# Expert weights asked for one block sooner, and the first blocks moved between the steps of routing

## The chip, the cores and the metric

The kernel runs on one core of one Trainium2 chip. The metric is the device time of one execution, in microseconds (us). A core has five engines with an instruction stream each: TensorE (PE, matmuls; its weight loads are PEld), VectorE (DVE), ScalarE (ACT), GpSimd (POOL) and SyncE (SP, which here issues nearly all DMAs; POOL issues the indirect ones). They wait for each other and for DMAs by semaphores.

## What is computed

Three layers follow each other on 2304 tokens: a retention layer (attention with decay), a dense layer of width 2048 with softplus, and a mixture of 8 experts of which each token uses two. The part that the change touches is the last:

```python
logits = x @ w_gate
noise_scale = np.log1p(np.exp(x @ w_noise))
noisy_logits = logits + noise_scale * noise
top2 = np.argpartition(-noisy_logits, 2, axis=1)[:, :2]
...
for e in range(E):
    for k in range(2):
        mask = top2[:, k] == e
        h = np.maximum(x[mask] @ w1[e], 0.0)
        out[mask] += top2_w[mask, k, None] * (h @ w2[e])
```

Which token goes to which expert is known only on the chip, while the kernel runs.

## The kernel before, in words

**Precision.** Every fp32 operand of a large matmul is split into two fp16 parts, and three products are summed. An expert's weights, so split, take 2 MB per half (w1 and w2, 128 partitions x 8192 fp16 each). They are prepared early on and stored in DRAM (`wsc`).

**Layers one and two** run through six tiles of 384 tokens: `g1` (line 281) and `g2` (line 312) alternate on TensorE. `logits` (line 403) and `ranks` (line 444) route a tile once it is done and scatter each token's number and weight into a table in DRAM.

**Blocks.** The experts' work is cut into blocks of 128 rows, each of one expert. `schedule` (line 496) computes on VectorE which expert each block has. It runs twice: list a, from the first five of six tiles, gives the first 5 blocks (`NBA`); list b gives the rest once the last tile is routed. A list holds for each block its column of the table, the place of its weights, its expert, and whether the expert is new.

**One block** i passes through these steps. `prep` (line 613): POOL copies the block's token numbers out of the loaded table (`ti`) and gathers the rows (`xr`), and SP transposes them by DMA (`xt`). `weights(i, half)` (line 600): SP reads three numbers of the list into registers and starts a load that is skipped where the expert isn't new. `e1` (line 628): 2 x 12 matmuls into `ph`; ScalarE and VectorE write the two fp16 parts `hr`; SP transposes them (`ht`). `e2` (line 648): 24 matmuls into `py`. `combine` (line 659): ScalarE scales `py` into `y`, POOL adds it to the output by an indirect DMA. `place` (line 596) reads the place of the weights into a register of TensorE.

**Order.** TensorE runs `e1(i)` and then `e2(i-3)`. After `ht` of block i, SP asks for the w1 of block i+3 and the w2 of block i, both of which TensorE reaches three blocks later. Weights have three places, used in turn by successive experts; line 681 lets a load for block n begin when block n-3 has finished its matmuls. Experts are taken large, small, large, small, so that a small one hides behind a large one. The first five blocks take PSUM from a pool in which `py` has one buffer and `ph` two (`eps`), the later ones from a pool with two of each (`eps2`). 41 blocks are in the main loop; if the routing makes more, two more run one after the other behind a branch (line 815).

The instructions are put into each engine's stream by a scheduler that follows the order in which they are written, moves one forward where it expects another to wait, and keeps what `behind` and `issue_after` tie together.

Of the kernel before, what the change touches and what calls it, by code (L numbers as in the profile page):

```python
# [10 lines left out]
F32 = mybir.dt.float32  # L11
F16 = mybir.dt.float16
I32 = mybir.dt.int32
# [4 lines left out]
ALU = mybir.AluOpType  # L18

B, H, S, D = 4, 8, 576, 64  # L20
NT, DM, FF = 2304, 512, 2048
NE, F2 = 8, 1024
P = 128
# [3 lines left out]
NTILE = NT // TT  # L27
KC = DM // P
NFB = FF // P
NBLK = 2 * NT // P + NE - 1  # L30
NB = NT // P
NBA = 5
NTAIL = 2
NCOL = NE * NB + NBLK

BIG = 4096
ROW = (slice(0, 64), slice(64, 128))
# [38 lines left out]
def body(ctx, tc, ins, out):  # L76
# [264 lines left out]

    X2 = dram.tile([NT, 2 * DM], F16, name="X2")
    table = dram.tile([P * NCOL, 4], I32, name="table")
    init = rt.tile([P, 17, 4], I32, name="init")
    nc.gpsimd.memset(init[:, :, 0:1], 0)
    nc.gpsimd.memset(init[:, :, 1:2], BIG)
    nc.gpsimd.memset(init[:, :, 2:4], 0)

    zero = rt.tile([P, DM // 4], F32, name="zero")
    nc.gpsimd.memset(zero, 0.0)  # L350

    def out_zero():
# [7 lines left out]
    wg = rt.tile([P, 2, KC, 16], F16, name="wg")  # L360

    def route_load():
        nc.sync.dma_start(out=table.rearrange("(p a c) f -> p a (c f)", p=P, c=17),
                          in_=init.rearrange("p (o c) f -> p o (c f)", o=1).to_broadcast([P, NCOL // 17, 68]))
        nc.sync.dma_start(out=noise, in_=ins["moe2_noise"].rearrange("(j p) e -> p j e", p=P))
        nc.sync.dma_start(out=wg32[:, :, 0:8], in_=ins["moe2_w_gate"].rearrange("(k p) e -> p k e", p=P))
        nc.sync.dma_start(out=wg32[:, :, 8:16], in_=ins["moe2_w_noise"].rearrange("(k p) e -> p k e", p=P))
        nc.scalar.activation(wg[:, 0], wg32, AF.Copy, scale=S_WG)
        nc.vector.scalar_tensor_tensor(out=wg[:, 1], in0=wg32, scalar=S_WG, in1=wg[:, 0], op0=ALU.mult, op1=ALU.subtract)
# [121 lines left out]

    POS = {}

    def schedule(first, n):
        X = mybir.AxisListType.X
        s = "a" if first else "b"

        def new(*shape, dt=F32, count=[0]):  # L500
            count[0] += 1
            return rt.tile([P, *shape], dt, name=f"sc{s}{count[0]}")

        def tt(shape, a, b, op, dt=F32):
            o = new(*shape, dt=dt)
            nc.vector.tensor_tensor(out=o, in0=a, in1=b, op=op)
            return o

        def ts(a, s1, s2, op0, op1=None, dt=F32):
            o = new(a.shape[1], dt=dt)  # L510
            nc.vector.tensor_scalar(o, a, s1, s2, op0=op0, **({"op1": op1} if op1 else {}))
            return o

        def red(a, op=ALU.add):
            o = new(a.shape[1])
            nc.vector.tensor_reduce(out=o, in_=a, axis=X, op=op)
            return o

        inner = lambda a, m: a[:, None, :].to_broadcast([P, m, NE])
        outer = lambda a: a[:, :, None].to_broadcast([P, a.shape[1], NE])  # L520
        eid, num = iota[:, :NE], iota[:, :n]
        pc = ps.tile([P, NE], F32, tag="sm", name="pc", bufs=1)
        nc.tensor.matmul(pc, lhsT=ones, rhs=MC[NTILE - 1 if first else NTILE][:, 0], start=True, stop=True)
        ni = ts(pc, 0.0 if first else 127.0, None, ALU.add, dt=I32)
        nb = new(NE)
        nc.vector.tensor_copy(nb, ts(ni, 7, None, ALU.logical_shift_right, dt=I32))
        if first:
            key = new(NE)
            nc.vector.scalar_tensor_tensor(out=key, in0=pc, scalar=8.0, in1=eid, op0=ALU.mult, op1=ALU.subtract)
            pos = red(tt([NE, NE], inner(key, NE), outer(key), ALU.is_gt, F16))  # L530
            r1 = ts(pos, 2.0, None, ALU.mult)
            POS["pos"] = tt([NE], r1, ts(r1, -1.0, 15.0, ALU.mult, ALU.add), ALU.min)
            POS["done"] = None
        else:
            pos = POS["pos"]
            nb = tt([NE], nb, POS["done"], ALU.subtract)
        lt = tt([NE, NE], inner(pos, NE), outer(pos), ALU.is_lt, F16)
        some = ts(nb, 0.0, None, ALU.is_gt)
        before_b = red(tt([NE, NE], lt, inner(nb, NE), ALU.mult, F16))
        before_e = red(tt([NE, NE], lt, inner(some, NE), ALU.mult, F16))  # L540
        end = tt([NE], before_b, nb, ALU.add)
        last = ts(red(some[:, None, :]), -1.0, None, ALU.add)
        sel = tt([n, NE], outer(num), inner(before_b, n), ALU.is_ge, F16)
        sel = tt([n, NE], sel, tt([n, NE], outer(num), inner(end, n), ALU.is_ge, F16), ALU.subtract, F16)
        pick = lambda a: red(tt([n, NE], sel, inner(a, n), ALU.mult, F16))
        e = pick(eid)

        w = new(NE)
        nc.vector.scalar_tensor_tensor(out=w, in0=eid, scalar=float(NB), in1=before_b, op0=ALU.mult, op1=ALU.subtract)
        if not first:  # L550
            w = tt([NE], w, POS["done"], ALU.add)
        col = pick(ts(w, float(-NE * NB), None, ALU.add))
        bi = rt.tile([P, 4, n], I32, name="bi" + s)
        nc.vector.scalar_tensor_tensor(out=bi[:, 0], in0=col, scalar=float(NE * NB), in1=num, op0=ALU.add, op1=ALU.add)

        d = ts(pick(ts(before_e, last, None, ALU.subtract)), last, None, ALU.add)
        if first:
            POS["e"], POS["d"] = e[:, n - 1:n], d[:, n - 1:n]
            POS["done"] = tt([NE], ts(before_b, -1.0, float(n), ALU.mult, ALU.add), nb, ALU.min)
            nc.vector.tensor_scalar(POS["done"], POS["done"], 0.0, None, op0=ALU.max)  # L560
            nc.vector.memset(bi[:, 3, 0:1], 1)
        else:
            other = tt([1], e[:, 0:1], POS["e"], ALU.not_equal)
            nc.vector.tensor_copy(bi[:, 3, 0:1], other)
            d = ts(d, tt([1], other, POS["d"], ALU.add), None, ALU.add)
        three = tt([n], ts(d, 3.0, -3.0, ALU.is_ge, ALU.mult), ts(d, 6.0, -3.0, ALU.is_ge, ALU.mult), ALU.add)
        nc.vector.tensor_tensor(out=bi[:, 1], in0=three, in1=d, op=ALU.add)
        nc.vector.tensor_copy(bi[:, 2], e)
        nc.vector.tensor_tensor(out=bi[:, 3, 1:], in0=d[:, 1:], in1=d[:, :n - 1], op=ALU.is_gt)
        if not first:  # L570
            LIST["more"] = ni[0:1, 0:1]
            nc.vector.tensor_scalar(ni[:, 0:1], red(nb[:, None, :]), float(n - NTAIL), None, op0=ALU.is_gt)
        tab = E["ep"].tile([P, NCOL * 4], I32, name="tab", bufs=1)
        nc.sync.dma_start(out=tab, in_=table.rearrange("(p c) f -> p (c f)", p=P))
        return bi, tab
# [94 lines left out]
    def weight_deps():  # L670

        for W, M in ((W1, M1), (W2, M2)):
            for n, w in W.items():
                need(M[n][0], w)
                for i in (n - 1, n - 2):
                    if i >= 0:
                        for m in M[i]:
                            tc.declare_no_dep(w.ins, m.ins, reason="another place")
                            tc.declare_no_dep(m.ins, w.ins, reason="another place")
                if n >= 3:  # L680
                    need(w, M[n - 3][-1], mybir.DependencyReason.ANTI)
                for i in W:
                    if i < n:
                        tc.declare_no_dep(w.ins, W[i].ins, reason="another place, or an expert already used")
# [92 lines left out]
        step()  # L777
    for g in sorted(todo):
        run(g)
    logits(NTILE - 1)  # L780
    ranks(NTILE - 1)
    LIST["b"] = schedule(False, NBLK - NBA)
    ps_s.close()
    E["eps2"] = ctx.enter_context(tc.tile_pool(name="eps2", bufs=2, space=bass.MemoryType.PSUM, side="right"))
    LAG, AHEAD = 3, 3
    NMAIN = NBLK - NTAIL
    preps = list(range(PA, NMAIN))
    for i in range(NMAIN + LAG):
        j = i - LAG

        def second():
            e2(j)
            combine(j)
            if j + 3 < NMAIN:
                weights(j + 3, 1)

        early = i == NMAIN - 1
        if early:
            second()
        if i < NMAIN:  # L800
            e1(i)
            if i == 0:
                weights(i, 1)
            if i + 1 < NMAIN:
                place(i + 1)
            if i + 3 < NMAIN:
                weights(i + 3, 0)
        if j >= 0 and not early:
            second()
        while preps and preps[0] <= i + AHEAD + 1 and (preps[0] < NBA or i >= PB):  # L810
            prep(preps.pop(0))
            if preps and preps[0] == NBA + 2 and i == PB:
                break
# [36 lines left out]
```

## Time and profile before

| | us |
|---|---|
| median of 3 runs (lowest, highest) | 962.01 (955.81 to 967.28) |
| the profiled execution | 956.63 |
| its span in the trace | 954.8 |
| TensorE busy in the span | 907.2 (95%) |
| VectorE, ScalarE, GpSimd busy | 384.8, 375.3, 262.0 |
| mean granted TensorE clock | 0.982 |

TensorE is busy through most of the span, so time is to be found where it stands still or runs at a lower clock. The profiled execution lies near the lowest of the three runs. Rows of the trace name line and engine, then what is written `<-` what is read.

### The profile page before, as it was taken

Reading aid. Unit: us, or ns where it says so; the run is one execution under the profiler, and the core shown is the slowest. Engines: PE = TensorE matmul, PEld = TensorE weight load, DVE = VectorE, ACT = ScalarE, POOL = GpSimd, SP = SyncE. Lnnn points to the kernel's source line nnn. Section 1 sums busy time; section 2 is a strip of 40 time slices with the busy share of each in tenths; the row PEclk is TensorE's granted clock in tenths of the full one; section 3 lists DMA queues with packets and bytes.
Section 4 is the critical chain, followed back from the end, with each engine's and each line's share of the span. In section 5 each row is a group of like instructions: output and inputs, shape, how many; then the busy total and the mean of one; then the engine's idle time right before and its main releaser. Section 6 shows DMA issues by size and latency. Waiting matters only on the chain. (4 is left out here: it accounts for less than half of the span.)

```text
span 954.8 us, 17453 instructions
## 1 busy us (share of the span) xinstructions
PE 907.2 (95%) x5690; PEld 464.4 (49%) x5690; DVE 384.8 (40%) x757; ACT 375.3 (39%) x601; POOL 262.0 (27%) x237
## 2 busy tenths in 40 slices
PE   7788899999999999999997999999999999899996
PEld 6444455555555555555543444444444444344442
DVE  4576775777867876424445111111111111111100
ACT  2777774665766766344431111111111111111111
POOL 3367632401410310200222223223222322223112
PEclk8899998999999999999999999999999999999999
DMA  9768899999999999003067777799879999999873
GB/s 311 249 227 276 218 281 326 309 358 327 343 326 321 355 363 272 1 1 67 18 179 206 150 132 124 150 243 213 216 138 198 212 235 185 199 268 219 213 174 54
DMA packets 221428, 206.70 MB, mean 216 GB/s; under 512 B 159360, under 2 KB 169216, under 8 KB 219296
## 3 DMA queue, kind: packets, MB, share of 16 engines
q1 hardware_dynamic: 211008, 185.29, 69.7%
q0 software_dynamic: 10336, 20.27, 11.6%
q8 instruction: 54, 0.88, 0.4%
q14 instruction: 30, 0.25, 0.1%
HBM read 245.70 MB, written 54.20 MB: 314 GB/s over the span
## 5 line engine op out<-in xcount | busy, mean ns | idle before, releaser
L637 PE MATMUL ph<-w,xt 128*128 x984 | 223.4, 383 | 9.2 <-DMA w<-wsc 5.7
L654 PE MATMUL py<-w,ht 128*128 x984 | 219.2, 379 | 2.0 <-ACT y L665 1.9
L281 PE MATMUL pg<-x,wi 128*128 128x384 f16 x1152 | 208.7, 331 | 5.3 <-POOL wi L151 3.2
L312 PE MATMUL p<-w,g 128*128 128x512 f16 x864 | 203.8, 383 | 10.3 <-POOL w L151 8.3
L642 DVE SCALAR_TENSOR_TENSOR hr<-ph,hr 128x512 f16<-128x512 f32 x82 | 56.7, 691 | 361.0 <-ACT hr L641 346.9
L637 PEld LDWEIGHTS <-xt 128*128 128x128 f16 x984 | 96.7, 98 | 127.5 <-issue 15.3
L281 PEld LDWEIGHTS <-wi 128*128 128x128 f16 x1152 | 112.6, 99 | 92.4 <-issue 6.8
L654 PEld LDWEIGHTS <-ht 128*128 128x128 f16 x984 | 96.2, 98 | 118.7 <-issue 2.9
L666 POOL DMA_INDIRECT out_dram<-y,ti x41 | 65.3, 1592 | 303.0 <-ACT y L665 274.3
L312 PEld LDWEIGHTS <-g 128*128 128x128 f16 x864 | 81.2, 98 | 103.3 <-issue 14.6
L641 ACT ACTIVATE hr<-ph 128x512 f16<-128x512 f32 x82 | 49.0, 597 | 178.4 <-PE ph L637 176.6
L665 ACT ACTIVATE y<-py,ti 128x512 f32<-128x512 f32 x41 | 28.2, 687 | 187.1 <-PE py L654 182.6
L335 DVE SCALAR_TENSOR_TENSOR w<-w 128x1024 f16<-128x1024 f32 x64 | 86.0, 1347 | 30.0 <-ACT w L334 29.8
L334 ACT ACTIVATE w<-w 128x1024 f16<-128x1024 f32 x64 | 67.4, 1057 | 53.4 <-DMA wsc<-w 28.2
L290 ACT ACTIVATE r<-pg 128x384 f32<-128x384 f32 x96 | 46.6, 485 | 99.2 <-PE pg L281 99.0
L295 DVE SCALAR_TENSOR_TENSOR r<-a,r 128x768 f32<-128x768 f32 x48 | 49.0, 1021 | 75.0 <-ACT a L294 74.7
L482 POOL DMA_INDIRECT table<-tb,pos x36 | 41.8, 1160 | 124.7 <-DVE pos L467 99.9
L621 POOL DMA_INDIRECT xr<-X,ti x41 | 43.4, 1060 | 19.6 <-POOL ti L618 11.6
L210 POOL TENSOR_TENSOR w<-kv,w 96x512 f32<-96x512 f32 x19 | 21.0, 1107 | 98.6 <-PE pst L239 54.7
L291 ACT ACTIVATE a<-pg 128x384 f32<-128x384 f32 x96 | 46.6, 485 | 0.0
L213 POOL TENSOR_TENSOR w<-qk,w 128x384 f32<-128x384 f32 x20 | 24.5, 1226 | 66.7 <-PE px L258 45.4
L293 ACT ACTIVATE a<-a 128x768 f32<-128x768 f32 x48 | 40.3, 841 | 1.2
(126 smaller groups left out, 607.1 us busy)
## 6 DMA issues: line engine op xcount, KB each, us to landing
w<-wsc SPq DMA_DIRECT2D x78, 2048.0 KB
w<-in_moe_w_dram SPq DMA_DIRECT2D x64, 512.0 KB
wsc<-w SPq DMA_DIRECT2D x64, 512.0 KB
qk<-in_qk_dram SPq DMA_DIRECT2D x24, 384.0 KB
kv<-in_kv_dram SPq DMA_DIRECT2D x24, 384.0 KB
w<-in_moe_w_in_dram SPq DMA_DIRECT2D x8, 1024.0 KB
w<-in_moe_w_out_dram SPq DMA_DIRECT2D x8, 1024.0 KB
out_dram<-zero SPq DMA_DIRECT2D x1, 4608.0 KB
```

The source lines that it names most:

```text
L281: nc.tensor.matmul(pg, lhsT=wi[:, a, k, f * P:(f + 1) * P], rhs=x[:, b, k, :], start=n == 0, stop=n == 11)
L290: nc.scalar.activation(r[:, i], pg, AF.Relu, scale=S_G / sx)
L291: nc.scalar.activation(a[:, i], pg, AF.Abs)
L295: nc.vector.scalar_tensor_tensor(out=r, in0=a, scalar=S_G, in1=r, op0=ALU.mult, op1=ALU.add)
L312: nc.tensor.matmul(PG[t, j], lhsT=g[:, a, f % 2, j * P:(j + 1) * P], rhs=wo[b][:, f, :], start=f == 0 and a + b == 0, stop=f == NFB - 1 an ...
L334: nc.scalar.activation(h[:, 0], t, AF.Copy, scale=s)
L335: nc.vector.scalar_tensor_tensor(out=h[:, 1], in0=t, scalar=s, in1=h[:, 0], op0=ALU.mult, op1=ALU.subtract)
L637: M1[i].append(nc.tensor.matmul(ph, lhsT=xt[:, a * 4 + k, :], rhs=AR[0][:, ds(r * 8192 + (b * 4096 + k * 1024 + n * 512), 512)], start=m = ...
L641: LAST["act"] = nc.scalar.activation(hr[:, 0, n * 512:(n + 1) * 512], ph, AF.Relu)
L642: nc.vector.scalar_tensor_tensor(out=hr[:, 1, n * 512:(n + 1) * 512], in0=ph, scalar=0.0, in1=hr[:, 0, n * 512:(n + 1) * 512], op0=ALU.max ...
L654: M2[i].append(nc.tensor.matmul(py, lhsT=ht[:, a * 8 + c, :], rhs=AR[1][:, ds(r * 8192 + (b * 4096 + c * 512), 512)], start=len(M2[i]) == ...
L666: LAST["pool"] = nc.gpsimd.indirect_dma_start(out=out[:, :], out_offset=bass.IndirectOffsetOnAxis(ap=ti[:, 1:2], axis=0), in_=y[:, :], in_ ...
```

## The change

Four edits. (1) A load for block n is asked for one block sooner: w1 of block i+4 after `e1(i)`, w2 of block j+4 after `e2(j)`; it then waits for the matmuls of block n-4 instead of n-3. (2) List b gives each of the four largest experts at least two blocks if it has any left; the tail grows to three blocks, the table by some columns, and the modulo of the place by a term. There are still three places. (3) Blocks 0 to 2 are written between the steps of routing: `e1(0)` after `logits`, `e1(1)` after `ranks`, and `e1(2)` inside the second `schedule`, by the argument `between`. (4) Two small constant tiles move to a pool that is closed later on.

```diff
-NBLK = 2 * NT // P + NE - 1
+NBLK = 2 * NT // P + NE
-NTAIL = 2
-NCOL = NE * NB + NBLK
+NTAIL = 3
+NCOL = NE * NB + NBLK + 2
...
+            POS["least"] = ts(pos, 4.0, 1.0, ALU.is_lt, ALU.add)
...
             nb = tt([NE], nb, POS["done"], ALU.subtract)
+            nb = tt([NE], nb, tt([NE], ts(nb, 0.0, None, ALU.is_gt), POS["least"], ALU.mult), ALU.max)
...
         sel = tt([n, NE], sel, tt([n, NE], outer(num), inner(end, n), ALU.is_ge, F16), ALU.subtract, F16)
+        between()
...
+        three = tt([n], three, ts(d, 9.0, -3.0, ALU.is_ge, ALU.mult), ALU.add)
...
-                if n >= 3:
-                    need(w, M[n - 3][-1], mybir.DependencyReason.ANTI)
+                if n >= 4:
+                    need(w, M[n - 4][-1], mybir.DependencyReason.ANTI)
...
-    logits(NTILE - 1)
-    ranks(NTILE - 1)
-    LIST["b"] = schedule(False, NBLK - NBA)
...
+    def first(i):
+        e1(i)
+        place(i + 1)
+    logits(NTILE - 1)
+    first(0)
+    weights(0, 1)
+    weights(3, 0)
+    weights(3, 1)
+    weights(4, 0)
+    ranks(NTILE - 1)
+    first(1)
+    prep(preps.pop(0))
+    LIST["b"] = schedule(False, NBLK - NBA, lambda: first(2))
...
+    weights(5, 0)
+    weights(6, 0)
+    for i in range(2, NMAIN + LAG):
...
-            if j + 3 < NMAIN:
-                weights(j + 3, 1)
+            if j + 4 < NMAIN:
+                weights(j + 4, 1)
...
-            if i + 3 < NMAIN:
-                weights(i + 3, 0)
+            if i + 4 < NMAIN:
+                weights(i + 4, 0)
```

Two places of the streams, as they stand in the two kernels. VectorE before, towards the end of the second `schedule` (`scb...` are its intermediate values, `bib` is list b): the two `hr` rows of block 1 stand behind nearly all of it.

```order
L572 TENSOR_SCALAR scb1_5356<-scb34_5428 128x1
L564 CAST bib_5402<-scb28_5412 128x1
L506 TENSOR_TENSOR scb29_5415<-scb28_5412,sca31_4952 128x1
L642 SCALAR_TENSOR_TENSOR hr_5525<-ph_5526,hr_5525 128x512
L511 TENSOR_SCALAR scb30_5417<-scb27_5410,scb29_5415 128x38
L642 SCALAR_TENSOR_TENSOR hr_5525<-ph_5541,hr_5525 128x512
```

VectorE in the changed kernel: the same two rows stand at the beginning of the second `schedule`, right behind the positions (`pos`) that `ranks` computes, and the two of block 2 further on within it.

```order
L465 SCALAR_TENSOR_TENSOR qi_5428<-qi_5428 128x6
L467 SCALAR_TENSOR_TENSOR pos_5434<-qi_5428 128x6
L649 SCALAR_TENSOR_TENSOR hr_5460<-ph_5461,hr_5460 128x512
L512 TENSOR_SCALAR scb1_5521<-pc_5519 128x8
L649 SCALAR_TENSOR_TENSOR hr_5460<-ph_5476,hr_5460 128x512
L512 TENSOR_SCALAR scb3_5524<-scb1_5521 128x8
L527 CAST scb2_5523<-scb3_5524 128x8
```

What moved: block 1's two `hr` come ahead of the schedule's some 35 small operations instead of behind them, and what is left of the schedule comes behind them.

SP before, at the same point (`w2` is the load of block 0's second half, `tab` the table for list b):

```order
L645 DMA_TRANSPOSE ht_5468<-hr_5437 128x16x128
L609 ISA
L609 REGISTER_ALU
L609 DMA w2_85<-wsc_87 128x8192
L574 DMA tab_5431<-table_89 128x748
L605 TENSOR_LOAD bia_4944
```

SP in the changed kernel, later: the load of `tab` has moved behind the skipped loads of blocks 3 and 4 and behind the transposes of blocks 1 and 2.

```order
L616 DMA w1_84<-wsc_87 128x8192
L652 DMA_TRANSPOSE ht_5491<-hr_5460 128x16x128
L652 DMA_TRANSPOSE ht_5590<-hr_5559 128x16x128
L581 DMA tab_5648<-table_89 128x760
L612 TENSOR_LOAD bib_5615
```

What moved: the table is fetched later, behind two transposes that stood behind it; the load of block 0's second half still follows the transpose of block 0. Further on the two streams have the same pattern (transpose of `hr`, a load for each half, transpose of `xr`), with the loads belonging to one block later than before.

## Rows read from the trace of the kernel before

**Rows 1.** Waits of TensorE, 480 us to the end: engine, line, releaser: us, times, longest.

```profile
PE ph L637 <- DMA w<-wsc: 5.7, 3, 4.6
...
PE ph L637 <- DVE hr L642: 3.6, 1, 3.6
...
PE py L654 <- ACT y L665: 1.9, 2, 1.0
```

**Rows 2.** Timeline of TensorE, first blocks: start, us, engine, line, operation [idle before].

```profile
512.68 3.61 PE L637 MATMUL ph<-w,xt 128*128 x16
...
519.85 7.03 PE L637 MATMUL ph<-w,xt 128*128 x24 [3.56 <-DVE hr L642]
...
526.72 5.13 PE L654 MATMUL py<-w,ht 128*128 x23
...
538.29 2.75 PE L654 MATMUL py<-w,ht 128*128 x12 [1.05 <-ACT y L665]
...
549.64 1.02 PE L654 MATMUL py<-w,ht 128*128 x4 [0.83 <-ACT y L665]
```

**Rows 3.** Windows, core 0: PE, PEld, DVE, ACT, POOL busy, clock, DMA share, GB/s.

```profile
516.30:519.85 3.55, 0.00 (x0) 0.00 (x0) 3.55 (x16) 0.60 (x1) 2.64 (x4) 1.00 0.96 402
...
520.00:521.00 1.00, 1.00 (x5) 0.41 (x4) 0.97 (x5) 0.00 (x0) 0.81 (x1) 0.87 0.79 330
...
521.00:522.00 1.00, 1.00 (x4) 0.34 (x3) 0.31 (x2) 0.00 (x0) 0.89 (x1) 0.50 0.12 22
```

**Rows 4.** Timeline of TensorE, later blocks.

```profile
757.30 5.34 PE L637 MATMUL ph<-w,xt 128*128 x24 [0.30 <-DMA w<-wsc]
...
788.38 5.34 PE L637 MATMUL ph<-w,xt 128*128 x24
...
793.86 5.34 PE L654 MATMUL py<-w,ht 128*128 x24
...
824.55 7.00 PE L637 MATMUL ph<-w,xt 128*128 x24 [4.64 <-DMA w<-wsc]
...
831.39 5.34 PE L654 MATMUL py<-w,ht 128*128 x24
...
899.63 5.34 PE L637 MATMUL ph<-w,xt 128*128 x24 [0.74 <-DMA w<-wsc]
```

**Rows 5.** Timeline of SP's queue, later blocks.

```profile
735.62 0.64 SPq L609 DMA_DIRECT2D w<-wsc  x2
...
747.23 0.90 SPq L609 DMA_DIRECT2D w<-wsc  x2
...
798.58 2.00 SPq L645 DMA_TRANSPOSE ht<-hr  x1
...
812.76 0.94 SPq L609 DMA_DIRECT2D w<-wsc  x2
...
815.66 9.21 SPq L645 DMA_TRANSPOSE ht<-hr  x1
...
890.72 0.91 SPq L609 DMA_DIRECT2D w<-wsc  x2
```

**Rows 6.** Timeline of VectorE, end of the second schedule.

```profile
519.12 0.68 DVE L642 SCALAR_TENSOR_TENSOR hr<-ph,hr 128x512 f16<-128x512 f32 x1
...
521.11 0.23 DVE L567 TENSOR_TENSOR bib<-scb,scb 128x38 int32<-128x38 f32 x1
```

**Rows 7.** Timeline of SP and GpSimd, list b and block 5.

```profile
513.98 0.59 SPq L609 DMA_DIRECT2D w<-wsc  x1
...
523.27 0.32 SPq L574 DMA_DIRECT2D tab<-table  x1
...
526.13 0.19 POOL L618 COPY ti<-tab 128x4 int32 x1 [4.04 <-DMA tab<-table]
...
535.95 2.62 SPq L625 DMA_TRANSPOSE xt<-xr  x2
```

More of the change, by code (lines that the diff above doesn't have):

```diff
@@ L343, in body @@
     table = dram.tile([P * NCOL, 4], I32, name="table")
-    init = rt.tile([P, 17, 4], I32, name="init")
+    init = ap.tile([P, 19, 4], I32, name="init", bufs=1)
     nc.gpsimd.memset(init[:, :, 0:1], 0)
@@ L347, in body @@
     nc.gpsimd.memset(init[:, :, 2:4], 0)
-    zero = rt.tile([P, DM // 4], F32, name="zero")
+    zero = ap.tile([P, DM // 4], F32, name="zero", bufs=1)
     nc.gpsimd.memset(zero, 0.0)
@@ L362, in route_load @@
     def route_load():
-        nc.sync.dma_start(out=table.rearrange("(p a c) f -> p a (c f)", p=P, c=17),
-                          in_=init.rearrange("p (o c) f -> p o (c f)", o=1).to_broadcast([P, NCOL // 17, 68]))
+        nc.sync.dma_start(out=table.rearrange("(p a c) f -> p a (c f)", p=P, c=19),
+                          in_=init.rearrange("p (o c) f -> p o (c f)", o=1).to_broadcast([P, NCOL // 19, 76]))
         nc.sync.dma_start(out=noise, in_=ins["moe2_noise"].rearrange("(j p) e -> p j e", p=P))
@@ L494, in body, with schedule @@
     POS = {}
-    def schedule(first, n):
+    def schedule(first, n, between=lambda: None):
         X = mybir.AxisListType.X
@@ L674, in weight_deps @@
                 need(M[n][0], w)
-                for i in (n - 1, n - 2):
+                for i in (n - 1, n - 2, n - 3):
                     if i >= 0:
@@ L779, in body @@
         run(g)
-    logits(NTILE - 1)
-    ranks(NTILE - 1)
-    LIST["b"] = schedule(False, NBLK - NBA)
-    ps_s.close()
-    E["eps2"] = ctx.enter_context(tc.tile_pool(name="eps2", bufs=2, space=bass.MemoryType.PSUM, side="right"))
     LAG, AHEAD = 3, 3
@@ L787, in body @@
     preps = list(range(PA, NMAIN))
-    for i in range(NMAIN + LAG):
+    def first(i):
[11 more added lines that the diff above has]
+    LIST["b"] = schedule(False, NBLK - NBA, lambda: first(2))
+    ps_s.close()
+    E["eps2"] = ctx.enter_context(tc.tile_pool(name="eps2", bufs=2, space=bass.MemoryType.PSUM, side="right"))
+    weights(5, 0)
+    weights(6, 0)
+    for i in range(2, NMAIN + LAG):
         j = i - LAG
@@ L799, in body @@
             second()
-        if i < NMAIN:
+        if 2 < i < NMAIN:
             e1(i)
-            if i == 0:
-                weights(i, 1)
             if i + 1 < NMAIN:
                 place(i + 1)
-            if i + 3 < NMAIN:
-                weights(i + 3, 0)
+            if i + 4 < NMAIN:
+                weights(i + 4, 0)
         if j >= 0 and not early:
```

## The prediction, on record before the changed kernel ran

> **What bounds it now.** I read the page first: TensorE is busy for 95% of the span, so whatever is won must come from its pauses or from its clock. Then the list of TensorE's waits from 480 us on [rows 1]: three waits for an expert's weights, 5.7 us together, one of 3.6 us for VectorE, and two of 1.9 us together for ScalarE. Nothing else there is in reach of this change, so the prize is small from the start; the timelines show what each pause really costs.
>
> In the first blocks [rows 2], block 1's last matmuls start at 512.68 and end at 516.29. Block 2 starts only at 519.85: its PSUM buffer is freed by VectorE, whose `hr` of block 1 stands behind the second schedule and runs at 519.12 [rows 6]. TensorE has nothing else to do meanwhile, and when it starts again its granted clock is at the lower level, 1.2 GHz (0.50), where it was at 2.4 GHz (1.00) before the pause [rows 3]. So the group of 24 matmuls takes 7.03 us, against 5.34 in the later groups [rows 2, 4]. The reader should see that one pause is paid twice.
>
> In the later blocks [rows 4], groups of 24 last 5.34 us, but the last one overlaps its successor, and undisturbed starts follow each other by 5.18 us (5.34 less the 0.16 of overlap). Three experts' first blocks start late (757.30, 824.55, 899.63), with 0.30, 4.64 and 0.74 us of idle; the overlap that is lost adds 0.16 to each. The group at 793.86 follows the one at 788.38 by 5.48, thus 0.30 late. After the longest pause the clock is low again: 824.55 to 831.39 is 6.84, or 1.66 over 5.18.
>
> Why the weights are late stands in SP's queue [rows 5]. The loads come in pairs, one pair for each block. The pair that carries w1 of block 31 goes out at 812.76, 7 us before TensorE wants it. A transpose issued behind such a load takes 9.21 us instead of 2.00, so SP runs behind: from 747.23 to 890.72 are 13 pairs, 11.04 us each, against 10.36 (two groups of 5.18) for a block on TensorE.
>
> **The change, part by part.**
>
> *The first blocks.* VectorE now writes `hr` of block 1 as soon as it is there. Block 2 can start at 516.3, and its clock stays up. That removes 3.56 us and 7.03 - 5.34 = 1.69 us [rows 2]. The new order has one second matmul group directly behind another in the pool with a single `py` buffer, where it had two pauses for that buffer, 1.05 and 0.83 us: I keep the first and take away the second. Sum: 3.56 + 1.69 + 0.83 = 6.1 us.
>
> Two things could eat this. First, `e2(0)`, which now follows block 2, moves from 526.72 to about 516.3 + 5.2 = 521.5, and needs block 0's w2, issued at 513.98 [rows 7]. DMA moves 330 GB/s between 520 and 521 us and only 22 in the next [rows 3], so the load lands at about 521.1: just in time. The bounds are nothing lost, and 526.5 - 521.5 = 5 us lost, since before it had landed when `e2(0)` started. I take nothing, by the drop in traffic.
>
> Second, what is left of the schedule waits for two further `hr` of block 2, and list b, ready at 521.3 [rows 6], is ready about 5 us later, 526.6 by my count of its operations. Block 5 hangs on it: from `ti` at 526.13 to `xt` at 535.95 was 9.8 us [rows 7]. Now POOL first adds block 0's output, so `ti` comes near 530 and `xt` near 540, with some 3 us until it has landed. In the new order of TensorE block 5 comes after five groups for blocks 3, 4, 0, 1 and 2 from 521.5, at about 548.5. A cover of some 5 us is left; if it is gone, what is missing is paid in full. The three further operations of the first schedule, and four of the second, cost 0.1 to 0.2 us each on VectorE; the latter are in the 526.6, the former shift a wait by less than 0.5 us, which I leave out.
>
> *The loads, one block sooner.* They make up 0.46 + 0.30 + (4.64 + 0.16 + 1.66) + 0.90 = 8.1 us [rows 4]. Are they soon enough? Up to 735.62 SP keeps up with TensorE, and so it gets the 6.1 us from the first blocks as well. From there the same pairs follow in the same mixture, one block sooner; that is 747.23 - 735.62 = 11.6 us [rows 5]. Block 31's w1 goes out at 812.76 - 11.6 - 6.1 = 795.1 and needs 824.55 - 812.76 = 11.8 us: 806.9. It is wanted at 819.75 - 6.1 - 0.8 = 812.9. Margin 6.0. Block 38's goes out at 890.72 - 17.7 = 873.0, needs 899.63 - 890.72 = 8.9, so 881.9; wanted at 898.73 - 6.1 - 7.2 = 885.4. Margin 3.5, or 0.6 if it needs 11.8 too. So all four go, with little to spare at the end.
>
> What is not free is the place in the queue. Each load now stands ahead of the transpose of an older block than before, and a transpose behind a load takes 9.21 us instead of 2.00 [rows 5], 7.2 more. The transpose of block 29, out at 824.87, is used three blocks later, at 841.75 or so (819.75 + 4.80 + 1.66 + 3 x 5.18), with 17 us of cover; the shift takes 7.2 of that, the gain of TensorE over SP's queue up to 7.2 more. That leaves 2 to 3 us, so I cost it at nothing. The Trainium skill, "DMA: Bandwidth & Descriptors", section "Queues, rings and completion order", says that on each DMA engine a queue's descriptors are consumed in ring order. By that rule alone the transposes pay for what the loads win, and the sum would be that of the rival "transposes late" below; the trace agrees with the order (9.21 against 2.00 us), but not with there being no cover.
>
> *At least two blocks for a large expert; three tail blocks.* The reference, run on its own inputs, gives the eight experts 148, 573, 208, 22, 292, 1614, 1033 and 718 tokens, so 2 + 5 + 2 + 1 + 3 + 13 + 9 + 6 = 41 blocks, with a new expert at blocks 13, 14, 23, 25, 31, 33 and 38; the late ones of [rows 4] are three of these. The four largest have 8, 9, 6 and 5 blocks in list b, so the rule adds none, the list stays at 41 and the tail is jumped over as before: nothing. The table's columns and the two moved constants: nothing, they are written in the first microsecond or moved by DMA beside matmuls.
>
> **Sum.** 6.1 + 8.1 = 14.2 us, against the profiled execution's 956.63: 942.4, or 1.5% less. The median of the runs, 962.01, lies 5.4 higher; what those runs lost I cannot see, so I subtract the same: 947.8, rounded to **948 us**.
>
> **The rivals.**
>
> *Weights still late, or SP the next bound.* For: SP needs 11.04 us a block where TensorE needs 10.36 [rows 4, 5], 13 x 0.68 = 8.8 us over that stretch, so a queue that is behind can give back what the earlier asking wins. Against: the margins above. If 5 of the 8.1 remain, 962.0 - 9.2 = 952.8.
>
> *The first blocks win nothing.* The wait for VectorE is replaced by one for block 0's w2 or for block 5's rows. For: covers of 0.4 and 5 us only. Then 962.0 - 8.1 = 953.9.
>
> *Both, in part*, or the pauses of the profiled execution are not those of the other runs: 957 to 963, no change.
>
> *Transposes late: slower.* Each load pushes a transpose by 7.2 us; where the cover of 17 us in the later blocks is used up, `e2` waits at each load and the clock falls after it. It decides once SP is 17 us further behind TensorE than now. Then the seven loads among those 13 pairs would cost 7 x 7.2 = 50 us less the 14.2 won: 962 + 36 = 998; two more than the win, 963 to 975, are likelier than all.
>
> *The change does not do what it says:* extra blocks run the tail. With 41 blocks counted it cannot for these inputs; I give it 0.01, within the case of slower.
>
> **Chances and range.** Forecast 0.60 (944 to 952); weights or SP 0.15; first blocks 0.10; both in part 0.09; slower 0.06. The range must hold 0.8: the forecast, most of the next two, and 2 us less than the forecast's lowest if the other runs' extra 5.4 us lie in these same pauses (962.0 - 14.2 - 5.4 = 942.4). So 941 to 957. About 1% is what a measurement of this kernel can tell from no change, so faster means under 952.4: 0.58 of the forecast's 0.60, and half of the next two, 0.12, together 0.70. Slower by over 1% is 0.05 of the 0.06. Within 1%: the remaining 0.25.
>
> **What would show it.** In the new trace: no idle at block 2's first matmuls and a clock of 1.00 there; `e2(0)` at about 521.5 with no wait for `w<-wsc`; block 5 unhindered; no wait for `w<-wsc` at blocks 25, 31 and 38; pairs in SP's queue about 17 us sooner than before late in the list. Wrong if a wait of `py` for `ht` appears in the later blocks, if list b delays block 5, or if the time saved at these places is lost in the first 480 us, where I predict no difference.

## The result and the profile after

The changed kernel takes **948.72 us**, the median of 6 runs (944.47 to 952.0); the kernel before, run beside it, 961.75 (6 runs). The ratio is 0.9851, with a 95% interval of 0.9813 to 0.9889: 1.5% faster, as forecast to the microsecond. The traces show that the forecast was luckier than its working: what it counted went, but of its 14.2 us some 9.4 came back elsewhere in the execution that was profiled. (A run more than 1.5% above the fastest of its kernel is left out of the ratios in this document, not out of the medians.)

That execution took 951.07 us, 2.4 above the median of its runs; the one of before lay 5.4 below its median. So the two traces differ by 5.6 us only, and the medians by 13.0. From the first block's first matmul to the end of the span they differ by 6.0 (453.65 and 447.6 us).

First the waits of TensorE from 480 us on, after (compare [rows 1]; columns as there):

```profile
PE ph L644 <- DMA xt<-xr: 3.9, 1, 3.9
...
PE py L661 <- DMA ht<-hr: 1.3, 1, 1.3
PE py L661 <- issue: 1.2, 1, 1.2
PE py L661 <- ACT y L672: 0.8, 1, 0.8
```

All three waits for weights are gone, the one for VectorE's `hr` and one of the two for ScalarE too. New are waits for the two transposes, `xt` and `ht`, which no row of before has. Their places, in TensorE's timeline after:

```profile
512.17 4.04 PE L644 MATMUL ph<-w,xt 128*128 x18
...
516.08 5.34 PE L644 MATMUL ph<-w,xt 128*128 x24
522.62 5.34 PE L661 MATMUL py<-w,ht 128*128 x24 [1.21 <-issue]
527.80 10.52 PE L644 MATMUL ph<-w,xt 128*128 x48
...
544.34 5.34 PE L661 MATMUL py<-w,ht 128*128 x24 [0.84 <-ACT y L672]
549.51 10.52 PE L644 MATMUL ph<-w,xt 128*128 x48
...
851.45 5.34 PE L661 MATMUL py<-w,ht 128*128 x24 [1.33 <-DMA ht<-hr]
...
861.80 5.34 PE L661 MATMUL py<-w,ht 128*128 x24
871.06 7.94 PE L644 MATMUL ph<-w,xt 128*128 x24 [3.91 <-DMA xt<-xr]
878.84 1.46 PE L661 MATMUL py<-w,ht 128*128 x6
...
894.38 5.34 PE L644 MATMUL ph<-w,xt 128*128 x24
```

Block 2 follows block 1 with no pause, in 5.34 us where it took 7.03 after 3.56 of idle [rows 2]. `e2(0)` starts 1.2 us late. Blocks 5 and 6 (549.51) are not held up. `e1(38)`, the first block of the last new expert, starts at 894.38 with no wait. At 851.45 `e2(31)` waits for its `ht`; at 871.06 `e1(36)` for its `xt`, and its 24 matmuls then take 7.94 us: the clock is paid a second time, as at block 31 before [rows 4]. The clock's side, in the windows over block 2 and over `e1(36)` (columns as in [rows 3]):

```profile
516.08:521.42 5.34, 5.34 (x26) 2.25 (x24) 4.50 (x20) 1.20 (x2) 4.12 (x5) 1.00 0.86 349
871.06:878.84 7.78, 7.78 (x25) 3.01 (x25) 0.69 (x1) 0.60 (x1) 2.68 (x3) 0.66 1.06 160
```

1.00 is 2.4 GHz; the mean of 0.66 comes from a first part at 1.2 GHz (0.50 in the windows up to 876 us). And SP's queue after (compare [rows 5]):

```profile
794.49 1.10 SPq L616 DMA_DIRECT2D w<-wsc  x2
...
832.31 9.18 SPq L652 DMA_TRANSPOSE ht<-hr  x1
...
853.86 1.15 SPq L616 DMA_DIRECT2D w<-wsc  x2
855.13 1.40 SPq L632 DMA_TRANSPOSE xt<-xr  x1
856.63 13.98 SPq L652 DMA_TRANSPOSE ht<-hr  x1
873.15 0.64 SPq L616 DMA_DIRECT2D w<-wsc  x2
...
881.13 0.91 SPq L616 DMA_DIRECT2D w<-wsc  x2
```

Block 31's w1 goes out at 794.49 (812.76 before), 18.3 us sooner. Block 38's goes out at 881.13 (890.72 before), only 9.6 us sooner. The pair of 873.15 is the one before it, and both its loads are skipped: SP's queue moves 0.79 MB from 872 to 881 us, less than one load of 2 MB, and 2.73 MB from 881 to 892. For the two late transposes, these are the rows of the kernel before, of SP's queue and of the TensorE steps that read them:

```profile
837.31 7.10 SPq L645 DMA_TRANSPOSE ht<-hr  x1
...
862.40 1.26 SPq L625 DMA_TRANSPOSE xt<-xr  x1
```

```profile
862.47 5.34 PE L654 MATMUL py<-w,ht 128*128 x24
...
878.01 5.34 PE L637 MATMUL ph<-w,xt 128*128 x24
```

After, the `xt` of block 36 comes behind the pair of 853.86. It is asked at 855.13 and is there when TensorE goes on, at about 871: 16 us. TensorE's step before it ended at 861.80 + 5.34 = 867.1. The `ht` of block 31, asked at 832.31, took until about 851.4. Before, these two were asked at 862.40 and 837.31: the change brings them forward by 7.3 and 5.0 us, the load of block 31 by 18, and TensorE would reach the two steps 11.0 and 12.5 us sooner than before (`e1(36)` stood at 878.01, `e2(31)` at 862.47; now due at 866.98 and 849.95).

The DMA packets show where the 16 us of `xt` go. A load moves in large packets and a transpose in small ones. From 856.4 to 862 us only 10 of 144 packets were under 512 bytes, and SP's queue moved 1.79 MB; from 862 to 871 us it was 2109 of 2319, and the queue moved 0.81 MB. So the transposes asked at 855.13 and 856.63 stood still for some 7 us while the load asked just before them moved, and needed the next 9 us for themselves.

### The profile page after: what moved, and what is told of

Same layout as the page of the kernel before. It is cut to its first block, busy times and chain, and to the rows that moved or that the text cites. A ratio compares the mean times of both kernels' runs of the same rounds, so it can differ in the third digit from the quotient of the medians.

```text
span 949.0 us, 17456 instructions
## 1 busy us (share of the span) xinstructions
PE 908.7 (96%) x5690; PEld 466.8 (49%) x5690; DVE 385.1 (41%) x765; ACT 375.3 (40%) x601; POOL 265.8 (28%) x237
## 5 line engine op out<-in xcount | busy, mean ns | idle before, releaser
L335 DVE SCALAR_TENSOR_TENSOR w<-w 128x1024 f16<-128x1024 f32 x64 | 81.2, 1273 | 34.4 <-ACT w L334 33.0
L482 POOL DMA_INDIRECT table<-tb,pos x36 | 46.3, 1287 | 126.5 <-DVE pos L467 117.3
L293 ACT ACTIVATE a<-a 128x768 f32<-128x768 f32 x48 | 40.4, 841 | 1.2
L294 ACT ACTIVATE a<-a 128x768 f32<-128x768 f32 x48 | 40.3, 839 | 1.0
```

Source lines behind the costliest of these rows:

```text
L335: nc.vector.scalar_tensor_tensor(out=h[:, 1], in0=t, scalar=s, in1=h[:, 0], op0=ALU.mult, op1=ALU.subtract)
```

## The experiments

Each ran beside the kernel before on one chip. The diffs are shortened; - is the changed kernel and + the experiment. Of the letters in the expectations, D is throughout the theory that a transpose asked beside a load is late by that load, Q that SP's queue as a whole is the next bound.

**1 and 2. Each part alone.** Only the new order of the first blocks, with the loads three blocks ahead as before:

```
-                if n >= 4:
-                    need(w, M[n - 4][-1], ...)
+                if n >= 3:
+                    need(w, M[n - 3][-1], ...)
...
-            if j + 4 < NMAIN:
-                weights(j + 4, 1)
+            if j + 3 < NMAIN:
+                weights(j + 3, 1)
...
-            if i + 4 < NMAIN:
-                weights(i + 4, 0)
+            if i + 3 < NMAIN:
+                weights(i + 3, 0)
```

> The first blocks stand between the steps of routing as in the change, but the weights are asked for three blocks ahead as before. Theory A (each of the two parts brings its own term): the pause before block 2 and the low clock after it are gone, about 5 us less than before in time, some 956 to 957; the waits for weights at blocks 25, 31 and 38 are still there, and not smaller. Theory B (the earlier asking only turns waits for weights into waits for transposes, and the whole win is the order's): as fast as the changed kernel, 13 us less than before.

And only the loads four ahead, the first blocks behind the whole schedule as before:

```
-    LIST["b"] = schedule(False, NBLK - NBA, lambda: first(2))
+    LIST["b"] = schedule(False, NBLK - NBA)
...
-    for i in range(2, NMAIN + LAG):
+    for i in range(NMAIN + LAG):
```

> Weights asked for four blocks ahead as in the change, but the first blocks written in the order of before. Theory A: 8 us less than before, some 953, no wait for weights in the later blocks, and the pause of 3.6 us before block 2 with the low clock after it still there. Theory B: no difference to before (within 0.5%), with waits for transposes in the later blocks that make up for the weights.

Measured: the order alone 956.1 us, ratio 0.9949 (0.9909 to 0.9990); the loads alone 953.16, ratio 0.9925 (0.9888 to 0.9962); before 960.73. By the medians that is 4.6 and 7.6 us, and 12.2 together, against 13.0 for the whole change: the parts add up within the intervals, as theory A had it. (Both kernels keep edits 2 and 4 of the change; no run has those alone.) The 7.6 are what is left of the loads' gain after the new waits for transposes. The waits say the same. Order only (TensorE, from 480 us):

```profile
PE ph L644 <- DMA w<-wsc: 6.3, 3, 4.5
...
PE py L661 <- DMA w<-wsc: 1.7, 1, 1.7
```

Loads only:

```profile
PE ph L644 <- DMA xt<-xr: 6.5, 2, 5.2
PE ph L644 <- DVE hr L649: 4.2, 1, 4.2
...
PE py L661 <- DMA ht<-hr: 0.8, 1, 0.8
```

With the order alone the later blocks still wait for weights and for no transpose, and the `py` of block 0 waits 1.7 us for block 0's w2. With the loads alone the wait for `hr` stays, no weights are late, and `xt` is. So the new waits belong to the loads, not to the order.

**3. No loads.** All blocks keep the first expert's weights; this leaves out the other experts' weights, and with them part of the computation. SP still reads the numbers and evaluates the condition; TensorE takes place 0 and not the place in its register, and its groups of 24 last 5.34 us as before.

```
-  ... cond=(c == 1))
+  ... cond=(c == (1 if i == 0 else 2)))
...
-        ep, r, xt = E["ep2"], REG[i], XE.pop(i)
+        ep, r, xt = E["ep2"], 0, XE.pop(i)
...
-        r, ht = REG[i], HT.pop(i)
+        r, ht = 0, HT.pop(i)
```

> The changed kernel with none of the 14 loads of a later expert's weights: all blocks use the first expert's, so this leaves out part of the computation. It shows what the loads cost in all. Theory A (transposes are late in the later blocks because they stand behind a load): no wait for a transpose in the later blocks, SP's transposes take about 2 us each, and the profiled execution is 8 us shorter than that of the changed kernel, some 943; by the median 5 to 8 less. Theory C (SP's queue is late by its own pace, loads or not): the same waits for transposes, no faster than the changed kernel.

Measured: 940.64 us (936.31 to 942.79), ratio 0.9788 (0.9738 to 0.9838). No wait for `xt` or `ht` is left, and a transpose of `ht` in SP's queue looks like this:

```profile
800.37 1.98 SPq L652 DMA_TRANSPOSE ht<-hr  x1
```

The median of such rows between 560 and 890 us is 1.98 us, against 4.89 in the changed kernel. Theory A holds: the changed kernel still pays for its loads, by way of the transposes and the clock after them. It is 8 us by the medians, 6 by the two ratios to the kernel before; the intervals of these ratios overlap, so the size is rough.

**4. A longer round on SP.** Three more register reads for each block, their values unused.

```
+                if i:
+                    for k in (2, 1, 3):
+                        nc.sync.value_load(entry(i, k), min_val=0, max_val=NE - 1)
```

> The changed kernel with three more register reads on SP for each block, which are not used; a round of SP's queue then takes about 2 us more. Theory C (SP's pace is the bound in the later blocks): up to 2 us more for each of the about 20 blocks from block 20 on, 20 to 40 us slower than the changed kernel. Theory A (SP is late only behind loads, and makes up for it between them): some us slower, less than 10, from transposes that come later behind loads.

Measured: 991.51 us, ratio 1.0332 (1.0276 to 1.0388): some 43 us over the changed kernel, above even theory C's range, for reads that nobody needs. TensorE's waits:

```profile
PE ph L647 <- DMA xt<-xr: 31.2, 11, 5.9
PE py L664 <- DMA ht<-hr: 2.0, 1, 2.0
```

The shortest gap in SP's queue between the end of `ht` and the next load grows from 2.16 to 3.87 us, 1.7 a round (the expectation of experiment 10 says 2.1). SP then no longer makes up between the loads what it loses beside them, and 12 steps of TensorE wait where 2 did. It shows how little is left: SP's queue is the next bound behind the weights.

**5. The kernel before, a second trace.** Unchanged, one execution.

> The kernel before, unchanged, for a second profile. Its profiled execution was 5 us under its median, that of the changed kernel 2 us above. If the first 480 us make the difference between executions, the waits for weights here are again some 8 us with the low clock, and the first block's matmuls start some us earlier or later than 501.15. If the waits for weights differ from one execution to the next, they are larger here, 12 us or more.

Measured: 963.53 us, 6.9 more than the first profiled execution. Its late weights:

```profile
758.23 5.34 PE L637 MATMUL ph<-w,xt 128*128 x24 [1.18 <-DMA w<-wsc]
...
824.14 7.03 PE L637 MATMUL ph<-w,xt 128*128 x24 [3.39 <-DMA w<-wsc]
...
904.23 8.15 PE L637 MATMUL ph<-w,xt 128*128 x24 [5.28 <-DMA w<-wsc]
```

The idle is 9.85 us, the lost overlap 3 x 0.16, the slow clock 1.69 + 2.81 (7.03 and 8.15 less 5.34): 14.8 us, where the same count gave 8.1 in the first execution. The two stages differ by 8.2 us, of which this is 6.7. So the waits for weights differ between these two executions, and the first was the milder. Late weights of this size can account for the 5.4 us that the forecast could not see; that they do, two executions can't show.

**6. The loads on another queue.** From block 6 on ScalarE asks for the weights, so the transposes have SP's queue for themselves.

```
-        with behind("sync"):
+        q = nc.scalar if 5 < i < NBLK - NTAIL else nc.sync
+        with behind("act" if q is nc.scalar else "sync"):
...
-            w = nc.sync.dma_start(...)
+            w = q.dma_start(...)
```

> The changed kernel with the loads of blocks 6 to 40, and their three register reads, on ScalarE's queue instead of SP's; the transposes stay on SP. Theory C' (SP's one queue is the bound late in the list: a round of it takes 8 us, 13 to 14 with a load): SP is left with two transposes a block, no wait for a transpose remains, and it is as fast as the kernel without loads, some 941. Theory D (the DMA engines themselves are full behind a load, whichever queue asks): transposes still take 7 to 9 us behind a load and the waits for them stay, 946 to 949.

Measured: 8 runs, four from 940.0 to 949.8 us and four from 965 to 992; the ratio, 0.9861 (0.9809 to 0.9913), is that of the first four, and it does not tell C' from D. The traced execution, at 984 us, is one of the other four. Its waits and two rows of SP:

```profile
PE py L662 <- DMA ht<-hr: 37.8, 3, 22.3
PE ph L645 <- DMA xt<-xr: 3.5, 1, 3.5
```

```profile
822.51 20.16 SPq L653 DMA_TRANSPOSE ht<-hr  x1
...
850.71 14.10 SPq L653 DMA_TRANSPOSE ht<-hr  x1
```

With no load in SP's queue a transpose still kept SP busy for 20.16 us there. But from 825 to 831 us the DMA engines were busy for a share of 0.22 and moved 37 GB/s, so they were not full either. This execution fits neither theory, its cause is open, and no reading below rests on it.

**7. `xt` ahead of the weights.** In each round the next block's rows are asked before the loads.

```
-            if i + 4 < NMAIN:
-                weights(i + 4, 0)
-        if j >= 0 and not early:
-            second()
         while preps and ...:
             prep(preps.pop(0))
...
+        if 2 < i < NMAIN:
+            if i + 4 < NMAIN:
+                weights(i + 4, 0)
+        if j >= 0 and not early:
+            second()
```

> The changed kernel with the transpose of the gathered rows ahead of the loads in each round of SP's queue instead of behind them. The sum of SP's work is the same. Theory C': the wait for xt goes, since it is asked for some 4 us sooner and not directly behind a load, but ht is late instead by a part of it; 2 to 5 us faster than the changed kernel. If it is just the sum of SP's work that counts, no difference.

Measured: 943.35 us (936.45 to 949.34), ratio 0.9829 (0.9783 to 0.9876). In the profiled execution (936.45, the fastest of the six) the later blocks wait only once:

```profile
PE py L661 <- DMA w<-wsc: 1.1, 1, 1.1
PE py L661 <- ACT y L672: 0.8, 1, 0.8
PE py L661 <- DMA ht<-hr: 0.7, 1, 0.7
```

The first is `e2(0)`, with the cause in plain words: block 0's w2, where the changed kernel's row says "issue".

**8. Five blocks ahead.** If weights still bound anything, a further block would win again.

```
-                if n >= 4:
-                    need(w, M[n - 4][-1], ...)
+                if n >= 5:
+                    need(w, M[n - 5][-1], ...)
...
-                weights(j + 4, 1)
+                weights(j + 5, 1)
...
-                weights(i + 4, 0)
+                weights(i + 5, 0)
```

> The changed kernel with weights asked for five blocks ahead instead of four. If weights are no longer late with four (no wait for them was left), this brings nothing: within 0.3% of the changed kernel, with the same waits for transposes. If in other executions weights are still late, some us faster.

Measured: 954.36 us (941.46 to 970.37), ratio 0.9889 (0.9821 to 0.9957): nothing won over four. In the later blocks TensorE waits for transposes alone:

```profile
PE ph L644 <- DMA xt<-xr: 7.8, 4, 3.1
PE py L661 <- DMA ht<-hr: 2.6, 1, 2.6
```

**9 to 12. What is left, side by side on one chip.** The changed kernel again (9), with one register read for a block in place of three (10), with the order of 7 (11), with both (12). The one read takes a number that VectorE packs:

```
+        nc.vector.scalar_tensor_tensor(out=bi[:, 2], in0=bi[:, 1], scalar=8.0, in1=bi[:, 2], ...)
+        nc.vector.scalar_tensor_tensor(out=bi[:, 3], in0=bi[:, 2], scalar=2.0, in1=bi[:, 3], ...)
...
-                WR[i] = (nc.sync.value_load(entry(i, 2), ...), nc.sync.value_load(entry(i, 1), ...) if i else 0,
-                         nc.sync.value_load(entry(i, 3), ...))
+                v = nc.sync.value_load(entry(i, 3), min_val=0, max_val=47)
+                sl = nc.s_assert_within(v >> 4, 0, 2, ...) if i else 0
+                WR[i] = ((v >> 1) & 7, sl, v & 1)
```

> The changed kernel once more, beside the three kernels of this call on one chip, so that they can be compared with it and not only with the kernel before. If the waits behind loads are what is left (theory D: a pair of transposes asked right behind a load is held up by it), they turn up again among blocks 25 to 38, for xt or ht, at 4 to 9 us with the clock lost behind them, perhaps at other blocks than 31 and 36. If those two waits were an accident of one execution, there is none. Median by either: 946 to 951.

> Expert, place and the flag of a new load packed into one number by two VectorE instructions per list, so that SP reads one register value a block and not three; TensorE's order is the changed kernel's to the row. Three more reads lengthened a round by 2.1 us, so two fewer should shorten it by about 1.4. Theory Q (SP's queue as a whole is the next bound, every round counts): SP reaches block 36's xt 10 us or more sooner, since the blocks from 25 on save 1.4 us each; the wait of 3.9 us there goes, and of the stage 3 to 6 us: 943 to 946. Theory D (only the transposes right behind a load are late, by the load itself): the waits stay at a few us, within 2 us of the changed kernel: 947 to 950.

> The order of the earlier run once more (in a round xt asked ahead of the weights), beside the changed kernel on the same chip. If that order's gain was real, 3 to 6 us under the changed kernel, 943 to 946, and no wait for xt. If it was the chip of that call, the same as the changed kernel within 2 us.

> Both: xt asked ahead of the weights, and one register read in place of three. Theory Q: nothing is left of the queue's cost, the blocks run as without loads: 939 to 943, no wait for xt, ht or weights but block 0's 1.2 us. Theory D: ht still stands behind loads, and waits of 1 to 3 us for it stay: 943 to 946.

The medians of 6 runs each, before 960.28. The third column is worked out from the runs (ratio of the means, 2.3 standard errors to either side); idle is 340 us less TensorE's busy time in the windows from 560 to 900 us of the one profiled execution:

| kernel | us | against the changed kernel (9) | idle of TensorE, us |
|---|---|---|---|
| 9, changed kernel again | 945.72 | | 10.7 |
| 10, one read | 943.99 | 0.9967 (0.992 to 1.001) | 2.3 |
| 11, `xt` first again | 945.70 | 0.998 (0.992 to 1.004) | 3.7 |
| 12, both | 940.07 | 0.9930 (0.988 to 0.998) | 0.4 |

The traced execution of 9, 953.64 us, is the slowest of its six and that of 10, 941.10, the fastest, so the last column sets 9 too far from 10. The changed kernel's second trace shows that its new waits are no accident, nor bound to one block: (9, TensorE)

```profile
664.80 5.34 PE L644 MATMUL ph<-w,xt 128*128 x24 [2.21 <-DMA xt<-xr]
...
839.47 7.03 PE L661 MATMUL py<-w,ht 128*128 x24 [2.33 <-DMA ht<-hr]
849.45 7.03 PE L644 MATMUL ph<-w,xt 128*128 x24 [2.95 <-DMA xt<-xr]
874.30 7.03 PE L644 MATMUL ph<-w,xt 128*128 x24 [2.29 <-DMA xt<-xr]
```

874.30 is `e1(36)` once more; 664.80 is block 17, sooner than expected, and each wait is shorter than the 4 to 9 us expected. With two shorter waits (0.52 and 0.42) the six idle for 10.7 us, lose 3 x 1.69 to the clock and 6 x 0.16 of overlap: 16.7 us, twice what the first trace shows. With one read (10) `e1(36)` still waits, but the clock holds:

```profile
863.18 5.34 PE L646 MATMUL ph<-w,xt 128*128 x24 [1.70 <-DMA xt<-xr]
869.13 5.34 PE L663 MATMUL py<-w,ht 128*128 x24 [0.60 <-DMA ht<-hr]
```

SP's shortest gap between `ht` and the next load falls from 2.17 to 1.29 us, 0.9 and not the 1.4 that I expected, and its total does not add up: block 36's `xt` is asked 352.6 us after the first block's first matmul (847.69 less 495.04), against 353.7 in the changed kernel (855.13 less 501.40). So "10 us sooner" was wrong: between loads SP catches up and stands waiting for `hr`. (It waits for `hr` between 780 and 890 us for 22.0 and 29.3 us in the two traces of the changed kernel, 37.4 in 10.) Neither theory holds alone. My reading, argued and not shown: what counts is the burst, some rounds with loads close behind each other, in which D makes each transpose late and SP's own work decides whether the cover lasts. The time of 10 alone can't be told from 9. Nor can that of 11, so the gain that 7 seemed to have over the changed kernel is not confirmed; its one wait is for weights:

```profile
PE ph L644 <- DMA w<-wsc: 3.7, 1, 3.7
```

That is block 38's, which in this order stand behind one more transpose. Both together (12) leave nothing in the later blocks but this:

```profile
870.14 5.34 PE L663 MATMUL py<-w,ht 128*128 x24 [0.44 <-DMA ht<-hr]
```

940.07 us is about the time of the kernel without loads (940.64), and 0.7% under the changed kernel, with an interval that does not reach 1. Against before it is 0.9794 (0.9745 to 0.9842).

## Why the prediction was right, and where it was not

*First blocks, 6.1 us.* The pause and the slow clock went to the letter: block 2 at 516.08, clock 1.00. (One reading was off, at no cost: by [rows 3] the clock before was still 1.00 in the pause and 0.87 from 520 to 521 us, so it fell after TensorE had begun again.) One of the two waits for `py` went. `e2(0)`, costed at no wait because block 0's w2 would land at 521.1, started at 522.62. Asked at 513.90, the load thus took 8.7 us until TensorE went on, not 7.1. The traffic drops between 520 and 522 us here too (347 and 22 GB/s), so the drop was not yet the moment at which TensorE can go on. Within the bound of 5, and 1.2 us off. Block 7's `e1` starts 5.3 us sooner than before, and the order alone measured 4.6.

*List b and block 5.* List b was ready at 526.93 + 0.20 = 527.1, forecast 526.6. Block 5's `ti` came at 535.64, some 5.6 later than forecast, but its `xt` was asked at 540.89, forecast 540, and block 5 was not held up: the cover of 5 us held.

*Loads, 8.1 us.* No weights are late in the changed kernel's two traces. Block 31's pair went out at 794.49, forecast 795.1. Block 38's went out at 881.13, 8.1 us later than the forecast 873.0: SP did not keep there what the working gave it. TensorE itself was 8.2 us late by then, from the waits for transposes, and took up `e1(38)` at 894.38. Without these waits it would have been due at about 886.2, while the load, with the 8.9 us that it needed before, is there at 890.0: an estimate, by which one late load was hidden by late transposes, and the margin of 3.5 us was gone. In experiment 11 just this load is late, by 3.7 us. The loads alone measured 7.6, net of the waits for transposes that they bring.

*Transposes, costed at nothing.* **This step failed.** The working had 17 us of cover for `ht`, less 14.4, and from "2 to 3 us" left it took nothing. Its own sign of being wrong appeared: a wait of `py` for `ht` in the later blocks. In the changed kernel's trace TensorE waits 1.33 and 3.91 us for transposes and loses 2.60 to the clock (7.94 less 5.34) and 2 x 0.16 of overlap: 8.2 us, as much as the loads' term. And the later and dearer of the two was `xt`, of which the working did not speak: it stands right behind a pair of which one is a load, takes 16 us, and is wanted by the very next steps. The Trainium skill ("DMA: Bandwidth & Descriptors", "Queues, rings and completion order") says that on each DMA engine a queue's descriptors are consumed in ring order. The trace agrees: hardly a small packet ran until the load ahead had moved, some 7 us. The rival's size, one late transpose for each of seven loads, was too large: two were late in the first trace, six, by 0.42 to 2.95 us, in the second.

*Why the total came out right all the same.* I subtracted from the median what I had found in a mild execution of before. Another execution loses more to late weights (14.8 us in experiment 5), and the change removes that too. This gain, not counted, stood against the loss, not counted. The runs bear out both: without loads the changed kernel is some 20 us under before (experiment 3) where 14.2 were counted, and its loads cost it 6 to 8. Their sizes are loose. Two executions of before lost 8.1 and 14.8 us to late weights, two of the changed kernel 8.2 and 16.7 to transposes, and the latter two lay 2.4 and 7.9 us above their medians. That gain and loss cancel to the microsecond is luck.

*What stays open.* The first block's first matmul starts at 501.15 and 499.84 in two executions of before, and between 493.14 and 501.40 in twelve of the changed kernel and its variants (mean 496.8). TensorE's order there is the same. The spread goes with the granted clock between 100 and 200 us: 0.95 in the two executions that start after 501 us, one of each kernel, and 1.00 in the five that start before 495.1. Whether 2 to 4 us of the 13.0 come from that stage, and whether edits 2 and 4 have a part in it, two executions of before can't tell. The packets show a transpose standing behind a load; why its own packets then run slower than without loads (2109 small ones in the 9 us from 862, against 3022 in the 4 us from 800 in experiment 3) was not separated.

*The rivals.* "SP the next bound" described a part of what happened (block 38's pair), with its price hidden in the median. "First blocks win nothing", "both, in part" and "slower" are out; "slower" had its mechanism right, and experiment 4 shows it at work with 1.7 us more a round on SP.

## What to carry to other kernels

When a transfer is asked for sooner on a queue that others share, name the first thing that then stands behind it, and take its cover from the trace to the microsecond: here a cover of 2 to 3 us, taken for nothing, became a loss of 8. One profiled execution is a sample; where the median lies elsewhere, read a second one before a term is sized. A bound behind the bound is found by lengthening it on purpose: three useless register reads a block cost some 43 us.

## What the runs showed that I had not expected

- A transpose of `ht` asked behind a load of 2 MB keeps SP busy several times as long: 1.98 us with no loads (median), 5.4 to 14.0 behind the 14 loads of the changed kernel. From 620 us on the windows show the DMA share near 1.0 with loads (1.04, 0.91, 0.99, 1.04 in the changed kernel) and 0.64 to 0.71 without.
- A register read on SP is not free: gaps of 1.29, 2.16 and 3.87 us with one, three and six reads, about 0.4 to 0.6 each.
- Pauses of like length do not always cost TensorE its clock: after 2.15 us of idle the next 24 matmuls took 7.03 us, after 2.79 they took 5.34 (both in experiment 4).
